# Attention and two expert layers on one core: blocks ordered by pairs of sequences, the second layer's weights converted during the first layer's second block

## The chip, the cores and the metric

The kernel runs on one core of a Trainium2 chip. The time is the device time of one execution in microseconds (us); lower is better. The profiled execution has a span of its own, from its first to its last instruction. The engines are TensorE (PE in the rows, its weight loads PEld), VectorE (DVE), ScalarE (ACT), GpSimd (POOL) and SyncE (SP), which issues nearly all DMAs.

## What is computed

Four sequences of 576 rows, eight heads of width 64, then two layers of width 512 to 2048 and back:

```python
scores = q @ k.T / sqrt(64)
thresh = max(scores, row) - tau
attn = softmax(where(scores >= thresh, scores, -1e9))
x = concat_heads(attn @ v)                    # 2304 x 512
h = x @ moe_w_in                              # first layer
x = (h * clip(h + 3, 0, 6) / 6) @ moe_w_out
h = x @ moe2_w_in                             # second layer
out = max(h, 0) ** 2 @ moe2_w_out
```

The four weight matrices arrive as 64-bit floats, and the results are wanted in float32.

## The kernel before

**Precision.** TensorE multiplies halves: each float32 operand of the layers and of attn @ v is kept as a pair of float16 tiles (a head and the rest), and three products of them are summed. The scores of sequence 0 are plain float32 products (line 281, `u.plain`, set on line 182); those of sequences 1 to 3 use float32r tiles `q_st` and `k_st`, which `prep_steps` fills with a head and a rest of q and k (lines 210, 211, 220 and 221, and a copy by DMA on line 224) and whose products line 285 sums.

**Attention.** A unit is a pair of heads of one sequence, four units to a sequence, nine jobs to a unit: one job is 128 query rows against 576 keys (the ninth takes the last 64 rows of both heads). `scores` fills a PSUM tile, `soft1` takes the row minimum on VectorE (291), the threshold, and the exponent on ScalarE (301); `soft2` applies the threshold on VectorE (308), rounds on ScalarE (314), takes the rest on GpSimd (315, 316) and has a DMA transpose it (318); `av`, `LAG` = 5 steps later, multiplies by v. A generator makes one such step at a time; `attn_to(n)` runs it up to step n.

**Layers.** A block is one layer of one sequence: 16 `hidden` steps and 16 `output` steps (four groups of four), each 24 matmuls with 288 columns (lines 655 and 692). Hidden PSUM tiles, output PSUM tiles and score tiles share one pool of three. Two yields follow each step, and the main loop calls `attn_to` at each, so that attention for the sequence that comes next is spread evenly over the yields that are left until it is needed (`ng`, line 776 onwards). At the end of a first-layer block the largest value of the result is found (line 700 to 707: VectorE, a small matmul, VectorE) and `split_scaled` makes the float16 pairs for the second layer from it.

**Order of blocks.** `blocks` on line 750: for each sequence the first layer, then the second. `BUBBLE` = 8 extra yields stand after a first-layer block, in which attention can run while the split is made. Between a second-layer block and the next sequence's first layer `before_last` finishes attention and calls `split_x`.

**Weights.** A weight unit is 256 rows or columns of a matrix, 32 units in all, used in the order of `wseq`. When sequence 0 needs a unit, `w_next` loads its 1 MB (499 or 502), takes the largest exponent per group of two units (518), makes float32 of the 64-bit words (581 and 589 on ScalarE, 590 on VectorE; the first four units use 584 and 585), rounds to float16 (592), takes the rest on GpSimd (593), and writes the pair to DRAM (595); sequences 1 to 3 read that back (572). `tick` asks for the units `LEAD` steps ahead of use. So both layers' weights are converted in blocks 1_0 and 2_0 (layer and sequence), while the attention of sequence 1 runs.

**Scheduling.** The order of the code gives priorities; the order on each engine is fixed when the program is built.

Of the kernel before, what the change touches and what calls it, by code (L numbers as in the profile page):

```python
# [26 lines left out]
SPLIT = 34  # L27
FIRST_DVE = 4
N_G, N_PT = 3, 5
NWD, N_W = 4, 4  # L30
LEAD = 8
BUBBLE = 8
# [4 lines left out]
def attention_moe_moe_kernel(  # L37
# [52 lines left out]
    q_st = [[big.tile([P, QZ], F32R, name=f"q_st{h}{i}") for i in range(2)] for h in range(2)]  # L90
    k_st = [[big.tile([P, 2, S], F32R, name=f"k_st{h}{i}") for i in range(2)] for h in range(2)]
    own = [slice(0, D), slice(D, 2 * D)]
    xr = [big.tile([P, S], F32, name=f"xr{c}") for c in range(NC)]
# [11 lines left out]
    q_pl = me.tile([P, 2, 2 * NT + 1, P], F32, name="ya", bufs=1)  # L105
    xh, xl = [None] * NC, [None] * NC
    xsc = {}

    def new_x(c):
        t = big.tile([P, 2, S], F16, tag=f"xh{c}", name=f"x16{c}")  # L110
        xh[c], xl[c] = t[:, 0], t[:, 1]
# [13 lines left out]
    def setup():  # L125
# [9 lines left out]
        nc.vector.memset(ones_r, 1.0)  # L135
        for h in range(2):
            nc.gpsimd.memset(q_pl[own[1 - h], :, h * NT:h * NT + NT], 0.0)
            nc.gpsimd.memset(q_pl[own[1 - h], :, 2 * NT, own[h]], 0.0)
        for h in range(2):
            for i in range(2):  # L140
                nc.gpsimd.memset(q_st[h][i][:, NT * P:NT * P + 64].bitcast(F32), 0.0)
                nc.gpsimd.memset(q_st[h][i][:, QZ - 64:].bitcast(F32), 0.0)
        for h in range(2):
            for i in range(2):
                nc.gpsimd.memset(k_st[h][i][own[1 - h], 1, :].bitcast(F32), 0.0)

# [33 lines left out]
    def prep_steps(u):  # L180

        u.plain = u.b == 0
        if u.plain:

            u.qf = q_pl[:, u.i % 2]
            u.kf = xr[2 + u.i % 2]
# [15 lines left out]
            return  # L202
        u.qs = [q_st[h][u.i % 2] for h in range(2)]
# [149 lines left out]
    def finish(u, half):  # L353
# [8 lines left out]
        direct = u.b == 0 and u.p == NC - 1  # L362
        if direct and half == 0:
            new_x(u.p)
        for r, c, src in parts:
            if direct:
                s = xsc["s"]
                nc.scalar.activation(out=xh[u.p][r, c], in_=src, func=AF.Copy, scale=s[r])
                nc.vector.scalar_tensor_tensor(out=xl[u.p][r, c], in0=src, scalar=s[r], in1=xh[u.p][r, c], op0=ALU.mult, op1=ALU.subtract)
            else:  # L370
                nc.scalar.activation(out=xr[u.p][r, c], in_=src, func=AF.Copy)

    def split_scaled(src, s, cs=range(NC)):
        for c in cs:
            new_x(c)
            nc.scalar.activation(out=xh[c], in_=src[c], func=AF.Copy, scale=s)
            nc.vector.scalar_tensor_tensor(out=xl[c], in0=src[c], scalar=s, in1=xh[c], op0=ALU.mult, op1=ALU.subtract)  # L377

    def split_x(b, cs=range(NC)):
        s = xsc["s"] = st.tile([P, 1], F32, name="sx", bufs=2)  # L380
        e = st.tile([P, 1], F32, name="ex", bufs=2)
        nc.vector.tensor_reduce(out=s, in_=vscs[b], axis=AX.X, op=ALU.min)
        nc.vector.reciprocal(out=e, in_=s)
        xsc["e"] = e
        split_scaled(xr, s, cs)
# [34 lines left out]
    def run(us, all_jobs, pr):  # L420
        n = len(all_jobs)
        for i in range(n + LAG):
# [17 lines left out]
            if 0 <= x < n:  # L440
# [42 lines left out]
    n_ld = [0]  # L483
    n_sp = [0]
    w16s = {}
    scaled = {}

# [3 lines left out]
    def w_load():  # L491

        k = n_ld[0]
        src, kind, u, layer, b = wseq[k]
# [10 lines left out]
    def group_scale(k):  # L505

        src, kind, u, layer, b = wseq[k]
# [41 lines left out]
    def norm_scale(q):  # L549
# [3 lines left out]
        ops = [(u, j) for u in range(q * n, q * n + n) for j in range(UW // P)]  # L553
        for i, (u, j) in enumerate(ops):
            w = w_hl[wuse[("2_0", "i", u)]][:, 0, j * P:j * P + P]
            nc.tensor.matmul(a[:, 0:P], lhsT=w, rhs=w, start=i == 0, stop=i == len(ops) - 1)
        am = st.tile([P, 1], F32, name="gm", bufs=2)
        nc.vector.tensor_reduce(out=am, in_=a[:, 0:P], axis=AX.X, op=ALU.max)
        nc.vector.tensor_scalar(out=am, in0=am, scalar1=2.0 ** -40, scalar2=None, op0=ALU.max)  # L559
        m = all_max(am, ident_g)  # L560
        c = slice(q, q + 1)
# [4 lines left out]
    def w_next():  # L566
        k = n_sp[0]
        n_sp[0] += 1
        src, kind, u, layer, b = wseq[k]
        if b:  # L570
            w = new_w(kind)
            nc.sync.dma_start(out=w, in_=w16s[(layer, kind, u)])
            w_hl[k] = w
            return
# [4 lines left out]
        c = wt.tile([P, UW], F32, name="wc", bufs=2)  # L579
        t = wt.tile([P, UW], F32, name="wraw", bufs=2)  # L580
# [10 lines left out]
        w = new_w(kind)  # L591
# [4 lines left out]
        w16s[(layer, kind, u)] = dr  # L596
        w_hl[k] = w
        while n_ld[0] < len(wseq) and wseq[n_ld[0]][4] == 0 and len(w_raw) < NWD:
            w_load()
        n = NQ // UC  # L600
        if k + 1 < len(wseq) and wseq[k + 1][4] == 0 and wseq[k + 1][2] % n == 0:
            group_scale(k + 1)
        if layer == 2 and kind == "i" and u % n == n - 1:
            norm_scale(u // n)
# [17 lines left out]
    def moe(tag, layer, b, before_last):  # L622
# [47 lines left out]
        def output(qd):  # L670
# [151 lines left out]
```

## Time and profile of the kernel before

| | |
|---|---|
| median of 3 runs | 1113.68 us (1111.06 to 1116.08) |
| profiled execution | 1113.99 us, of it the span 1112.0 us |
| PE busy | 1014.1 us, 91% of the span |
| ACT, DVE, POOL busy | 656.2 us (59%), 645.1 us (58%), 501.1 us (45%) |
| DMA, mean share of 16 engines (queue q1) | 61.0% |
| granted TensorE clock, mean | 0.971 of full speed |

The shares are means over stages that differ. A stage is read from the busy times within its own window, set beside the length of that window; a window in which PE is busy throughout can only become shorter by less work for PE.

### The profile page before, as it was taken

How to read it: one execution, taken by the hardware profiler on the slowest of the kernel's cores; microseconds unless marked ns; L12 is line 12 of the kernel's file. 1: busy time of each engine (PE TensorE's matmuls, PEld its weight loads, DVE VectorE, ACT ScalarE, POOL GpSimd, SP SyncE). 2: the span in 40 equal slices, each digit the busy share in tenths (PEclk: the TensorE clock that was granted, in tenths of full speed). 3: DMA queues.
4: the chain of work that ended last, by engine and by line, in shares of the span. 5: the costliest groups of instructions: out<-in, count | busy, mean ns of one | idle time of the engine just before them, and what ended most of it. 6: DMA issues, size and time to landing. Idle time of an engine off the chain costs nothing.

```text
span 1112.0 us, 23377 instructions
## 1 busy us (share of the span) xinstructions
PE 1014.1 (91%) x9248; PEld 820.7 (74%) x9248; DVE 645.1 (58%) x1344; ACT 656.2 (59%) x1128; POOL 501.1 (45%) x613
## 2 busy tenths in 40 slices
PE   6666878898689899999999999999899999998998
PEld 4444666676578788888778888888788887776776
DVE  5878688788876765455765554555934241224122
ACT  6688699687698765655576555655554344313322
POOL 6677467565375743444354443344354212212111
PEclk9989999999799899999999999999999999998999
DMA  6999999888688775565666655656455442322211
GB/s 146 246 230 200 209 263 285 209 236 227 165 213 226 181 171 152 138 151 116 145 138 141 143 131 156 137 119 131 91 113 123 111 125 90 96 76 77 76 39 44
DMA packets 264126, 168.66 MB, mean 152 GB/s; under 512 B 221264, under 2 KB 233552, under 8 KB 264016
## 3 DMA queue, kind: packets, MB, share of 16 engines
q1 hardware_dynamic: 262688, 166.83, 61.0%
q8 instruction: 73, 1.20, 0.4%
q10 hardware_dynamic: 1328, 0.33, 0.1%
q14 instruction: 37, 0.30, 0.1%
HBM read 99.62 MB, written 21.50 MB: 109 GB/s over the span
## 4 chain that ended last, share of the span: by engine, by line
PE 69%; DVE 13%; DMA 9%; ACT 5%; issue 2%; POOL 1%; SPq 1%; DVEq 0%; ACTq 0%; POOLq 0%
PE y L692 29%; PE hp L655 28%; PE s L285 4%; PE o L340 3%; DMA wd<-in_moe_w_out_dram 3%; DMA wd<-in_moe_w_in_dram 3%; DVE wraw L590 2%; DVE nm L291 2%; DVE g L518 1%; DVE x L377 1%; DMA vraw<-in_v_dram 1%; PE tps L174 1%; PE s L281 1%; DVE e L308 1%; ACT wc L581 1%
## 5 line engine op out<-in xcount | busy, mean ns | idle before, releaser
L655 PE MATMUL hp<-x,wpi 128*128 128x288 f16 x3072 | 400.5, 288 | 12.6 <-DVE gm L559 4.2
L655 PEld LDWEIGHTS <-wpi 128*128 128x128 f16 x3072 | 298.6, 99 | 90.9 <-issue 9.0
L692 PEld LDWEIGHTS <-wpo 128*128 128x128 f16 x3072 | 299.3, 99 | 84.3 <-issue 5.4
L692 PE MATMUL y<-gh,wpo 128*128 128x288 f16 x2048 | 338.6, 289 | 7.6 <-DVE ya L698 4.0
L666 POOL TENSOR_TENSOR gl<-g,gh 128x576 f16<-128x576 f32 x128 | 167.4, 1309 | 297.8 <-ACT gh L665 294.3
L692 PE MATMUL y<-gl,wpo 128*128 128x288 f16 x1024 | 209.6, 288 | 0.0
L291 DVE TENSOR_REDUCE nm<-s 128x1 f32<-128x576 f32 x144 | 107.8, 751 | 65.8 <-PE s L285 59.4
L698 DVE SCALAR_TENSOR_TENSOR ya<-y,yq,ya 128x576 f32<-128x576 f32 (+1 forms) x97 | 77.9, 809 | 103.0 <-PE y L692 102.6
L316 POOL TENSOR_TENSOR p<-e,p 128x512 f16<-128x512 f32 x108 | 127.1, 1177 | 0.0
L665 ACT ACTIVATE gh<-g 128x576 f16<-128x576 f32 x128 | 86.9, 680 | 60.4 <-DVE g L663 32.0
L308 DVE SCALAR_TENSOR_TENSOR e<-s,thr,e 128x576 f32<-128x576 f32 x108 | 88.0, 815 | 38.4 <-ACT e L301 37.6
L285 PE MATMUL s<-k_st,q_st 128*128 128x288 f32 x480 | 95.2, 321 | 14.4 <-DVE mx L123 5.3
L340 PE MATMUL o<-v,pt 128*128 128x64 f16 (+1 forms) x2016 | 91.4, 200 | 12.0 <-DMA pt<-wpo 6.4
L314 ACT ACTIVATE p<-e 128x576 f16<-128x576 f32 x108 | 73.5, 681 | 47.9 <-DVE e L308 43.8
L340 PEld LDWEIGHTS <-pt 128*128 128x128 f16 x2016 | 80.9, 101 | 23.7 <-DMA pt<-wpo 9.6
L315 POOL TENSOR_TENSOR p<-e,p 128x64 f16<-128x64 f32 x108 | 39.0, 362 | 118.6 <-issue 82.7
L663 DVE TENSOR_TENSOR g<-g,hp 128x576 f32<-128x576 f32 x64 | 48.1, 751 | 70.8 <-ACT g L662 70.2
L659 ACT ACTIVATE g<-hp,r_h,aq 128x576 f32<-128x576 f32 x64 | 52.9, 828 | 55.1 <-PE hp L655 51.9
L285 PEld LDWEIGHTS s<-k_st,q_st 128*128 128x128 f32 x480 | 70.3, 192 | 18.8 <-issue 11.9
L660 DVE SCALAR_TENSOR_TENSOR g<-g,r_w,hp 128x576 f32<-128x576 f32 x64 | 51.7, 809 | 54.8 <-ACT g L659 54.7
L662 ACT ACTIVATE g<-hp,r_w 128x576 f32<-128x576 f32 x64 | 47.0, 734 | 58.0 <-PE hp L655 57.6
L301 ACT ACTIVATE e<-s,nm 128x576 f32<-128x576 f32 x108 | 78.4, 726 | 0.4
(124 smaller groups left out, 1084.8 us busy)
## 6 DMA issues: line engine op xcount, KB each, us to landing
wpi<-scr SPq DMA_DIRECT2D x48, 512.0 KB, 3.8
wpo<-scr SPq DMA_DIRECT2D x48, 512.0 KB, 3.9
wd<-in_moe_w_in_dram SPq DMA_DIRECT2D x16, 1024.0 KB, 6.9
wd<-in_moe_w_out_dram SPq DMA_DIRECT2D x16, 1024.0 KB, 7.0
scr<-wpi SPq DMA_DIRECT2D x16, 512.0 KB, 5.2
scr<-wpo SPq DMA_DIRECT2D x16, 512.0 KB, 5.7
kraw<-in_k_dram SPq DMA_DIRECT2D x16, 256.0 KB, 4.1
vraw<-in_v_dram SPq DMA_DIRECT2D x16, 256.0 KB, 3.3
```

Source lines behind the costliest of these rows:

```text
L285: nc.tensor.matmul(s[:, half, 0:HALF], lhsT=u.qs[sl][:, cs], rhs=u.ks[sl][:, kk, c], start=i == 0, stop=i == len(ops) - 1)
L291: nc.vector.tensor_reduce(out=j.nm, in_=j.s, axis=AX.XY, op=ALU.min)
L301: nc.scalar.activation(out=j.e, in_=j.s, func=AF.Exp, bias=j.nm, scale=-1.0)
L308: nc.vector.scalar_tensor_tensor(out=j.e, in0=j.s, scalar=j.thr, in1=j.e, op0=ALU.is_le, op1=ALU.mult, accum_out=u.sm[:, col:col + 1])
L314: nc.scalar.activation(out=p16[:, 0:S], in_=e, func=AF.Copy)
L316: nc.gpsimd.tensor_tensor(out=p16[:, S + TAIL:], in0=e[:, 0:NT * P], in1=p16[:, 0:NT * P], op=ALU.subtract)
L340: nc.tensor.matmul(o[:, n * w:n * w + w], lhsT=j.pt[:, c, :], rhs=vv[:, hs, vc, :], start=i == 0, stop=i == len(ops) - 1)
L655: nc.tensor.matmul(hp[:, a, 0:HALF], lhsT=wsl(tag, "i", f, w, c), rhs=x[c][:, a * HALF:(a + 1) * HALF], start=i == 0, stop=i == 3 * NC - 1)
L665: nc.scalar.activation(out=gh, in_=gf, func=AF.Copy)
L666: nc.gpsimd.tensor_tensor(out=gl, in0=gf, in1=gh, op=ALU.subtract)
L692: nc.tensor.matmul(a[:, k_, 0:HALF], lhsT=wsl(tag, "o", f, w, e), rhs=g[f][:, k_ * HALF:(k_ + 1) * HALF], start=i == 0, stop=i == len(ops) ...
L698: nc.vector.scalar_tensor_tensor(out=y, in0=av_, scalar=yq, in1=y, op0=ALU.mult, op1=ALU.add)
```

## The change

It reorders the blocks: both first layers of sequences 0 and 1, then both second layers, then the same for sequences 2 and 3. All attention of sequence 1 must therefore be done within block 1_0, that of sequence 2 within 1_1, 2_0 and 2_1, that of sequence 3 within 1_2; blocks 1_3, 2_2 and 2_3 have none beside them.

The second layer's weights are no longer converted when sequence 0 needs them: `convert` is called for one unit every 2.7 steps from step 34 on (`CONV`; block 1_1 starts at step 32), into a tile `wv` of its own with a single buffer, and only goes to DRAM; the second layer reads all its weights back, for sequence 0 too (16 more reads of 512 KB). Sequence 1's scores become plain float32 like those of sequence 0; the plain tiles and the float32r tiles share their memory, the latter being set up at sequence 2. Two sets of x tiles replace one; x of a sequence is split as soon as its third unit is finished, and the fourth unit's result is written split. `BUBBLE`, `SPLIT` and `before_last` go. Transposed tiles have 6 buffers in place of 5, raw weight tiles 3 in place of 4, and the conversion works in place in one tile (`wc`, 3 buffers). The norm of the second layer's input weights is taken unit by unit.

```diff
-SPLIT = 34
+CONV = (34, 2.7)
-N_G, N_PT = 3, 5
-NWD, N_W = 4, 4
+N_G, N_PT = 3, 6
+NWD, N_W = 3, 4
-BUBBLE = 8
...
+    def split_tiles(i):
         for h in range(2):
...
+            q_st[h][i] = big.tile([P, QZ], F32R, tag=f"qs{h}{i}", name=f"q_st{h}{i}")
+            k_st[h][i] = big.tile([P, 2, S], F32R, tag=f"ks{h}{i}", name=f"k_st{h}{i}")
...
-        u.plain = u.b == 0
+        u.plain = u.b < 2
...
-        direct = u.b == 0 and u.p == NC - 1
+        direct = u.p == NC - 1
...
+                    if j.last and j.u.p == NC - 2:
+                        split_x(j.u.b)
...
-        w = new_w(kind)
+        w = new_w(kind) if layer == 1 else wt.tile([P, 2, UW], F16, name="wv", bufs=1)
         nc.scalar.activation(out=w[:, 0], in_=t, func=AF.Copy)
         nc.gpsimd.tensor_tensor(out=w[:, 1], in0=t, in1=w[:, 0], op=ALU.subtract)
         dr = scr.tile([P, 2, UW], F16, name=f"scr{k}")
         nc.sync.dma_start(out=dr, in_=w)
...
+    def w_next():
+        k = n_sp[0]
+        n_sp[0] += 1
+        src, kind, u, layer, b = wseq[k]
+        if k < len(cseq) // 2:
+            w_hl[k] = convert()
+            return
+        w = new_w(kind)
+        nc.sync.dma_start(out=w, in_=w16s[(layer, kind, u)])
         w_hl[k] = w
...
+        while n_cv[0] < len(cseq) and n_cv[0] >= len(cseq) // 2 and CONV[0] + CONV[1] * (n_cv[0] - len(cseq) // 2) <= step:
+            convert()
...
-            if last and layer == 1 and b < B - 1:
-                for _ in range(BUBBLE):
-                    yield
...
-    blocks = [(f"{layer}_{b}", layer, b) for b in range(B) for layer in (1, 2)]
+    blocks = [(f"{layer}_{b}", layer, b) for p in range(0, B, 2) for layer in (1, 2) for b in (p, p + 1)]
...
+    cseq += [w for w in wseq if w[4] == 0]
```

The order on ScalarE within the first group of outputs of block 1_0, before: `ya` is an output step, `e` the exponent of a job, `wc` and `wpi` passes of a conversion, `q_st` the split of q.

```order
L696 ACTIVATE ya<-y,yq 128x576 x2
L592 ACTIVATE wpi<-wraw 128x1024
L220 ACTIVATE q_st_91<-tps,qs 64x64
L314 ACTIVATE p_2200<-e 128x576
L295 ACTIVATE thr<-nm,tau_a 128x1
L301 ACTIVATE e<-s,nm 128x576
L589 ACTIVATE wd<-wd 128x1024
L220 ACTIVATE q_st_93<-tps,qs 64x256
L581 ACTIVATE wc<-wd,sp 128x1024 x2
L696 ACTIVATE ya<-y,yq 128x576
```

The same place in the changed kernel:

```order
L723 ACTIVATE ya<-y,yq 128x576
L325 ACTIVATE p_2302<-e 128x576
L199 ACTIVATE k_pl_126<-tps 128x256
L199 ACTIVATE k_pl_126<-tps 128x320
L606 ACTIVATE wpo<-wc 128x1024
L306 ACTIVATE thr<-nm,tau_a 128x1
L312 ACTIVATE e<-s,nm 128x576
L606 ACTIVATE wpo<-wc 128x1024
L306 ACTIVATE thr<-nm,tau_a 128x1
L312 ACTIVATE e<-s,nm 128x576
L723 ACTIVATE ya<-y,yq 128x576
```

Between two outputs there were one job's exponent and the split of q; there are now two exponents, and k is only copied (`k_pl`). Of the conversion, two passes stand there where there were four.

The order on VectorE where the last sequence's first layer ends, before: `gm` to `sx` find the scale, `x` are the four splits, `g<-g,hp` on line 663 is the second layer's hidden step.

```order
L703 TENSOR_REDUCE gm<-y_13916 128x1
L118 TENSOR_REDUCE mx<-vm 128x1
L123 TENSOR_SCALAR ex<-mx 128x1
L707 RECIPROCAL sx<-ex 128x1
L629 TENSOR_TENSOR e_14051<-ex 128x1
L679 TENSOR_SCALAR yq<-e_y_109,e_14051 128x1 x3
L377 SCALAR_TENSOR_TENSOR x_14038<-ya,sx,x_14038 128x576
L377 SCALAR_TENSOR_TENSOR x_14041<-ya,sx,x_14041 128x576
L377 SCALAR_TENSOR_TENSOR x_14044<-ya,sx,x_14044 128x576
L377 SCALAR_TENSOR_TENSOR x_14047<-ya,sx,x_14047 128x576
L663 TENSOR_TENSOR g<-g,hp 128x576 x5
```

In the changed kernel sequence 2's first layer ends so, and the hidden steps between and behind (`g<-g,r_w,hp`) are sequence 3's first layer:

```order
L730 TENSOR_REDUCE gm<-y_11776 128x1
L687 SCALAR_TENSOR_TENSOR g<-g,r_w_97,hp 128x576
L121 TENSOR_REDUCE mx<-vm 128x1
L126 TENSOR_SCALAR ex<-mx 128x1
L734 RECIPROCAL s_11890<-ex 128x1
L656 TENSOR_TENSOR e_12924<-ex 128x1
L388 SCALAR_TENSOR_TENSOR x_11898<-ya,s_11890,x_11898 128x576
L388 SCALAR_TENSOR_TENSOR x_11901<-ya,s_11890,x_11901 128x576
L388 SCALAR_TENSOR_TENSOR x_11904<-ya,s_11890,x_11904 128x576
L388 SCALAR_TENSOR_TENSOR x_11907<-ya,s_11890,x_11907 128x576
L687 SCALAR_TENSOR_TENSOR g<-g,r_w_97,hp 128x576 x3
```

The splits moved from standing ahead of the hidden steps that need them to standing among the hidden steps of another sequence.

The order on ScalarE early in block 1_1 of the changed kernel (before, this block has no conversion beside it): `g` and `gh` are hidden steps, `wc` and `wv` the second layer's conversion.

```order
L686 ACTIVATE g<-hp,r_h,aq 128x576
L692 ACTIVATE gh<-g 128x576
L595 ACTIVATE wc<-wd,sp 128x1024 x2
L686 ACTIVATE g<-hp,r_h,aq 128x576
L606 ACTIVATE wv<-wc 128x1024
L306 ACTIVATE thr<-nm,tau_a 128x1
L312 ACTIVATE e<-s,nm 128x576
L221 ACTIVATE k_st_3497<-tps 64x320
L692 ACTIVATE gh<-g 128x576
```

The conversion's passes stand between the two ScalarE operations of hidden steps, in one in-order queue.

## Rows read from the trace of the kernel before

**Rows 1.** Busy time by stretch: start:end, length, then engines as the first line says

```profile
core 0: us, PE busy (x) PEld busy (x) DVE busy (x) ACT busy (x) POOL busy (x), PEclk, DMA share, GB/s
0.00:118.40 118.40, 78.94 (x657) 56.47 (x657) 89.95 (x211) 88.78 (x176) 80.37 (x153) 0.91 0.92 204
118.40:435.80 317.40, 275.92 (x2538) 224.21 (x2538) 241.12 (x517) 241.88 (x384) 183.46 (x187) 0.95 0.83 214
435.80:678.20 242.40, 237.20 (x2292) 197.03 (x2290) 140.54 (x298) 143.53 (x264) 103.81 (x128) 1.00 0.60 140
678.20:914.10 235.90, 232.48 (x2244) 192.80 (x2243) 121.27 (x246) 124.98 (x225) 92.59 (x113) 0.99 0.52 119
914.10:1112.00 197.90, 189.54 (x1524) 150.21 (x1522) 52.24 (x77) 56.99 (x79) 40.83 (x32) 0.98 0.23 73
```

**Rows 2.** The same view for seven quarters of blocks, and for the end

```profile
163.80:206.40 42.60, 34.12 (x302) 27.13 (x302) 36.99 (x72) 36.73 (x52) 31.25 (x29) 0.92 1.04 288
238.00:293.20 55.20, 40.12 (x357) 32.80 (x354) 45.77 (x98) 39.51 (x58) 29.86 (x33) 0.87 0.83 231
372.40:401.90 29.50, 29.50 (x292) 24.60 (x291) 19.24 (x43) 17.64 (x30) 19.85 (x21) 1.00 0.77 180
732.20:761.10 28.90, 28.90 (x286) 23.86 (x285) 15.00 (x30) 13.99 (x23) 13.90 (x17) 1.00 0.57 120
761.10:798.60 37.50, 35.56 (x370) 30.56 (x369) 27.81 (x67) 23.04 (x47) 14.34 (x21) 0.95 0.64 137
956.80:980.30 23.50, 23.50 (x194) 18.77 (x193) 6.53 (x8) 6.05 (x8) 5.10 (x4) 1.00 0.29 90
1081.10:1112.00 30.90, 26.01 (x213) 20.79 (x211) 7.98 (x11) 6.65 (x10) 3.83 (x3) 1.00 0.13 39
```

**Rows 3.** Lines 291 and 581 in five such quarters; last, 581 from 118.4 to 435.8

```profile
L291 DVE TENSOR_REDUCE nm<-s x5: 737/758/758, 164.5 to 199.6; 128x1 f32<-128x576 f32 x5
L581 ACT ACTIVATE wc<-wd,sp x6: 1225/1240/1255, 163.3 to 192.9; 128x1024 f32<-128x1024 f32 x6
L291 DVE TENSOR_REDUCE nm<-s x9: 740/747/758, 238.9 to 286.9; 128x1 f32<-128x576 f32 x9
L581 ACT ACTIVATE wc<-wd,sp x6: 1232/1244/1253, 238.9 to 276.1; 128x1024 f32<-128x1024 f32 x6
L291 DVE TENSOR_REDUCE nm<-s x5: 747/752/758, 376.3 to 401.7; 128x1 f32<-128x576 f32 x5
L581 ACT ACTIVATE wc<-wd,sp x2: 1229/1240/1252, 377.9 to 379.0; 128x1024 f32<-128x1024 f32 x2
L291 DVE TENSOR_REDUCE nm<-s x5: 747/748/758, 736.1 to 760.5; 128x1 f32<-128x576 f32 x5
L291 DVE TENSOR_REDUCE nm<-s x8: 737/747/757, 760.5 to 793.4; 128x1 f32<-128x576 f32 x8
L581 ACT ACTIVATE wc<-wd,sp x28: 1201/1237/1262, 137.4 to 379.0; 128x1024 f32<-128x1024 f32 x28
```

**Rows 4.** Groups of instructions by line: the three passes of one weight conversion on ScalarE

```profile
L581 ACT ACTIVATE wc<-wd,sp 128x1024 f32<-128x1024 f32 x32 | 37.9, 1234 | 0.2
L589 ACT ACTIVATE wd<-wd 128x1024 int32<-128x1024 uint16 x28 | 32.3, 1155 | 12.0 <-DMA wd<-in_moe_w_out_dram 8.4 <-DMA wd<-in_moe_w_in_dram 3.4
L592 ACT ACTIVATE wpi<-wraw 128x1024 f16<-128x1024 f32 x16 | 16.7, 1050 | 0.6 <-DVE wraw L590 0.6
```

**Rows 5.** Timeline of TensorE: eight float32 score records (281), eight of the split form (285)

```profile
33.13 2.11 PE L281 MATMUL s<-xr,ya 128*128 128x288 f32 x8
223.80 1.31 PE L285 MATMUL s<-k_st,q_st 128*128 128x288 f32 x8
```

**Rows 6.** Groups by line: VectorE's half of the split of q

```profile
L221 DVE SCALAR_TENSOR_TENSOR q_st<-tps,qs,q_st 64x256 fp32r<-64x256 f32 x72 | 30.0, 417 | 15.0 <-ACT q_st L220 13.0
```

**Rows 7.** Groups by line and DMA issues: the tail of a conversion

```profile
L593 POOL TENSOR_TENSOR wpi<-wraw,wpi 128x1024 f16<-128x1024 f32 x16 | 34.1, 2136 | 5.8 <-ACT wpi L592 5.4
scr<-wpi SPq DMA_DIRECT2D x16, 512.0 KB, 5.2
```

More of the change, by code (lines that the diff above doesn't have):

```diff
@@ L89, in attention_moe_moe_kernel @@
     QZ = NT * P + 3 * 64
-    q_st = [[big.tile([P, QZ], F32R, name=f"q_st{h}{i}") for i in range(2)] for h in range(2)]
-    k_st = [[big.tile([P, 2, S], F32R, name=f"k_st{h}{i}") for i in range(2)] for h in range(2)]
+    q_st = [[None] * 2, [None] * 2]
+    k_st = [[None] * 2, [None] * 2]
+    q_pl = [None] * 2
+    k_pl = [None] * 2
     own = [slice(0, D), slice(D, 2 * D)]
-    xr = [big.tile([P, S], F32, name=f"xr{c}") for c in range(NC)]
+    xr = [big.tile([P, S], F32, name=f"xr{c}") for c in range(NC - 1)]
     NG = NF // NQ
@@ L102, in attention_moe_moe_kernel, with new_x @@
     ident_g = const.tile([P, P], F32, name="ident_g")
[L105 to L111, printed above, removed]
+    X, xsc, xset = {}, {}, {}
+    def new_x(key, c):
+        if key not in X:
+            xset[key] = len(X) % 2
+            X[key] = [None] * NC, [None] * NC
+        t = big.tile([P, 2, S], F16, tag=f"x{xset[key]}{c}", name=f"x16{c}")
+        X[key][0][c], X[key][1][c] = t[:, 0], t[:, 1]
+        return X[key][0][c], X[key][1][c]
     def all_max(am, rhs=None):
@@ L483, in attention_moe_moe_kernel @@
     n_ld = [0]
+    n_cv = [0]
     n_sp = [0]
@@ L493, in w_load @@
         k = n_ld[0]
-        src, kind, u, layer, b = wseq[k]
+        src, kind, u, layer, b = cseq[k]
         n_ld[0] += 1
@@ L505, in group_scale @@
     def group_scale(k):
-        src, kind, u, layer, b = wseq[k]
+        src, kind, u, layer, b = cseq[k]
         n = NQ // UC
@@ L547, in group_scale, with norm_scale @@
         return sp
-    def norm_scale(q):
+    n2 = {}
+    def norm_scale(u, w):
         n = NQ // UC
         a = ps_a.tile([P, 512], F32, tag="acc", name="gr")
[L553 to L556, printed above, removed]
+        for j in range(UW // P):
+            v = w[:, 0, j * P:j * P + P]
+            nc.tensor.matmul(a[:, 0:P], lhsT=v, rhs=v, start=j == 0, stop=j == UW // P - 1)
+        if u % n == 0:
+            n2[0] = st.tile([P, n + 1], F32, name="n2", bufs=2)
+            nc.gpsimd.memset(n2[0][:, n:], 2.0 ** -40)
+        nc.vector.tensor_reduce(out=n2[0][:, u % n:u % n + 1], in_=a[:, 0:P], axis=AX.X, op=ALU.max)
+        if u % n < n - 1:
+            return
         am = st.tile([P, 1], F32, name="gm", bufs=2)
-        nc.vector.tensor_reduce(out=am, in_=a[:, 0:P], axis=AX.X, op=ALU.max)
-        nc.vector.tensor_scalar(out=am, in0=am, scalar1=2.0 ** -40, scalar2=None, op0=ALU.max)
+        nc.vector.tensor_reduce(out=am, in_=n2[0], axis=AX.X, op=ALU.max)
         m = all_max(am, ident_g)
-        c = slice(q, q + 1)
+        c = slice(u // n, u // n + 1)
         unit_of(m, m)
@@ L564, in norm_scale, with convert @@
         nc.vector.tensor_scalar(out=a_w[1][:, c], in0=m, scalar1=e_w[1][:, c], scalar2=2.0 ** 21, op0=ALU.mult, op1=ALU.mult)
[L566 to L570, printed above, removed]
-            w = new_w(kind)
-            nc.sync.dma_start(out=w, in_=w16s[(layer, kind, u)])
-            w_hl[k] = w
-            return
+    def convert():
+        k = n_cv[0]
+        n_cv[0] += 1
+        src, kind, u, layer, b = cseq[k]
         while n_ld[0] <= k:
@@ L596, in w_next @@
         w16s[(layer, kind, u)] = dr
-        w_hl[k] = w
[L598 to L604, printed above, removed]
+        while n_ld[0] < len(cseq) and len(w_raw) < NWD:
+            w_load()
+        if k + 1 < len(cseq) and cseq[k + 1][2] % (NQ // UC) == 0:
+            group_scale(k + 1)
+        if layer == 2 and kind == "i":
+            norm_scale(u, w)
+        return w
+    def w_next():
[4 more added lines that the diff above has]
+            w_hl[k] = convert()
+            return
+        w = new_w(kind)
+        nc.sync.dma_start(out=w, in_=w16s[(layer, kind, u)])
+        w_hl[k] = w
     def want_w(k):
@@ L779, in attention_moe_moe_kernel @@
                 break
-            ng += 4 * NF + (BUBBLE if t[0] == "1" else 0)
+            ng += 4 * NF
         start = steps[0]
-        xs = None
-        if i + 1 < len(blocks) and blocks[i + 1][1] == 1:
-            def xs(nxt=nxt, b=b):
-                attn_to(nxt + LAG)
-                split_x(b + 1)
-        for g, _ in enumerate(moe(tag, layer, b, xs)):
+        for g, _ in enumerate(moe(tag, layer, b)):
             if nxt is not None:
                 attn_to(min(nxt + LAG, start + math.ceil((nxt + LAG - start) * (g + 1) / ng)))
+        if i + 1 < len(blocks) and blocks[i + 1][1] == 1:
+            attn_to(nxt + LAG)
 _INS = ['q', 'k', 'v', 'tau', 'moe_w_in', 'moe_w_out', 'moe2_w_in', 'moe2_w_out']
```

77 lines of the change are left out of this document (38 added, 39 removed).

## The prediction

> **What bounds the kernel now.** The page's mean, TensorE busy for 91% of the span, hides two regimes, so I read busy times by stretch first: the start, then four pairs of blocks (both layers of one sequence) [rows 1]. The start, sequence 0's attention alone, takes 118.4 us with TensorE busy for 78.94 of it. The first pair takes 317.4 us and the second 242.4, though both do the same matrix work. The reader is to see the difference in the other columns: in the first pair ScalarE is busy for 241.88 us and VectorE for 241.12, against 143.53 and 140.54 in the second, because the weights of both layers are converted there. TensorE is busy for 237.20 of the second pair's 242.4 us and sets its length; in the first pair nothing is full, and everything waits a little for everything. The last pair has no attention and takes 197.9 us.
>
> Next come quarters of blocks, cut at every 192nd matrix product of the layers [rows 2], with two counts that tell what else ran in them [rows 3]. A bare quarter takes 23.5 us. With five jobs of attention it takes 28.9, TensorE being busy throughout: a job costs it (28.9 - 23.5) / 5 = 1.08 us. With eight jobs it takes 37.5, and TensorE is idle at times: (37.5 - 28.9) / 3 = 2.9 us for each job more. With five jobs and two conversions it takes 29.5, with five and six 42.6, with nine and six 55.2. So conversions cost 0.3 us each as long as TensorE is full, (42.6 - 28.9) / 6 = 2.3 us each when it isn't. In the quarters of 42.6 and 55.2 us the busiest engine, VectorE, is busy for 36.99 and 45.77 us, 87% and 83%. That share is my measure of how full such a mix gets.
>
> **The change, part by part.** The new order makes five stretches: the start; A, block 1_0 with all attention of sequence 1; B, blocks 1_1, 2_0 and 2_1 with that of sequence 2 and the second layer's conversion; C, block 1_2 with that of sequence 3; D, blocks 1_3, 2_2 and 2_3 alone.
>
> *The start.* The same steps come before the first block, and the same three units of weights are asked for: 118.4 us, as before. One raw weight buffer less and one transposed tile more I cost at nothing: what hides them is that a load is issued two units ahead; without it each late load would show as idle time of VectorE or ScalarE ahead of a conversion.
>
> *Plain scores for sequence 2 of the four.* Eight float32 records take 2.11 us on TensorE, eight of the split form 1.31 [rows 5], 0.264 and 0.164 us each with their ends. A unit has 36 of the one or 40 of the other: 9.5 against 6.6 us, so four units cost TensorE about 11.8 us more. In return VectorE loses its half of the split: for q alone 30.0 us over three sequences, 10 for one [rows 6], and the copies by DMA go.
>
> *A.* Its loop makes 41 steps of attention in one block where 128 yields used to share them. ScalarE's work is what it had in the first pair, 241.88 us, less a second-layer block (half of the last pair's 56.99, so 28.5), less the conversions that leave: 27 started in that stretch [rows 3], and of the first layer's 16 about 12 stay, so 15 go at 1.234 + 1.155 + 1.050 = 3.44 us [rows 4], 51.6. That leaves 162 us; VectorE loses the same parts and the split besides. At 86% full A takes 162 / 0.86 = 188 us. The bounds: 162, if ScalarE never waits; and by the slopes above, 10.25 jobs and 3 conversions a quarter, 4 x (28.9 + 5.25 x 2.9 + 3 x 2.3) = 204, with the 11.8 on top 216. I take 188, because the loaded quarters kept to that share with as many conversions and more.
>
> *B.* Twelve quarters with 3 steps of attention each: 12 x (23.5 + 3 x 1.08) = 321 us. The 16 conversions lie beside work of TensorE; at 0.3 us each B takes 326, at 2.3 us 358. There are about three to a quarter, between the cases of two and six, and their outgoing tile has one buffer; I take 1.2 us each, 340 us. The 16 reads more of 512 KB are hidden by the lead of eight steps.
>
> *C.* 31 jobs and the steps that trail them in four quarters, nearly eight to each: 4 x 37.5 = 150 us. The bounds: 4 x (23.5 + 7.75 x 1.08) = 127, if TensorE stays full; and the quarter with nine jobs and six conversions, less 2.3 for each of these, 4 x 41.4 = 166. I take the row that has the same mix. That row, TensorE at 35.56 of 37.5 us where it was full with five jobs, says that packing jobs costs only some 5% of TensorE's time. The Trainium skill (Perfetto Trace Analysis, section Optimization Strategy) speaks against the change here: a kernel whose most-contended engine changes from regime to regime may gain by interleaving the regimes, and this one takes attention out of three blocks and packs it into two. By that rule A and C would lie at their upper bounds, and the sum would be 44 us higher.
>
> *D.* Twelve bare quarters, and what the last one takes more than a bare one: 12 x 23.5 + (30.9 - 23.5) = 289.4 us, and 2.6 for the transposes of the other result: 292. The scale and the split between a sequence's two layers, which nothing covered in the last pair, now lie beside another sequence's hidden steps. Upper bound: one and a half times the last pair's 197.9, 297.
>
> *The sum.* 118.4 + 188 + 340 + 150 + 292 = 1088.4 us of span, with the 2.0 us that the profiled execution has around its span **1090 us**, against that execution's 1113.99; the median of the runs, 1113.68, is the same within 0.3 us, so nothing is shifted. The first two sequences go from 317.4 + 242.4 = 559.8 us to 528, the last two from 433.8 to 442: the gain is in taking 15 conversions out of a stretch where nothing is full and laying them under TensorE; a part is given back in C and by the plain scores.
>
> **The rivals.**
>
> 1. *Packed attention stalls TensorE (slower).* Scores, hidden and output tiles share three PSUM tiles, so a score tile that waits for VectorE holds up the next block step. At the upper bounds A is 216 and C 166: 1134 us. For it: the slope of 2.9 us a job, nearly three times TensorE's own 1.08. The Trainium skill's rule named above (Perfetto Trace Analysis, Optimization Strategy) would bring this. Against it: 95% in the quarter with eight jobs, and a VectorE that has less to do per job. It decides as soon as A and C together cost over 24 us more than forecast. Chance 0.16.
> 2. *The single outgoing buffer.* Rounding 1.05, the rest on GpSimd 2.14 and the landing of the write 5.2 us [rows 4, 7] make 8.4 us before the next conversion may round; 2.7 steps of B at 26.7 / 8 us are 9.0. Whatever delays one by over 0.6 us stops ScalarE, and behind it the hidden steps' own operations. At 2 us for each of 15 the time is 1120. Against it: stalls of ScalarE in single places are made up for as long as TensorE has a tile to go on with. Chance 0.10.
> 3. *Everything fits (faster still).* A at ScalarE's 162 and B at 326: 1050 us. For it: TensorE's own work in A is only 4 x 23.5 + 41 x 1.08 + 11.8 = 150 us; against it: no loaded quarter was over 87% full. Chance 0.14.
> 4. *The change doesn't do what it says*: the conversions could slip back behind their due times. The order has them in block 1_1. 0.02; about 1114 us.
>
> **How the numbers follow.** The forecast has a chance of 0.58, and by itself lies between 1072 and 1108, by A's share between 0.83 and 0.95 and B's conversions between 0.3 and 2.3. The range 1062 to 1124 takes in that, most of rival 2 and the nearer parts of 1 and 3. About 0.5%, 5.6 us, is what a measurement of this kernel can tell from no change. Faster than 1108 are most of the forecast and rival 3, with milder cases of rival 2: 0.68. The near misses of the forecast and of rival 2 make 0.13, rivals 1 and the worse half of 2, with what the forecast leaves over, 0.19.
>
> **What would show it.** In the changed profile: the start at 118 us; block 1_0 from its first matrix product of line 682 to the next block's in about 188 us, the busiest engine at 83 to 90%; block 1_1 to 2_1 near 340 with TensorE at 95% or more; 1_2 about 150; the last three blocks at 23.5 us a quarter without a gap. If A is over 212 us, or if ScalarE waits long before the rounding into `wv`, the forecast is wrong; if D isn't free of gaps, its simplest part is.

## The result and the profile after

The changed kernel takes 1122.05 us (median of 9 runs, 1116.47 to 1129.63), the one before 1111.83 us beside it (9 runs, 1107.31 to 1116.08): a ratio of 1.0088, 95% interval 1.0067 to 1.011. It is slower by 0.9%, where 1090 us and a gain were forecast: inside the range, near its upper end, on the side that had a chance of 0.19.

The changed kernel's page, busy time by engine (us, share of the span, instructions): by the sums of [rows 1], TensorE is busy for 12.6 us more than before and ScalarE for 10.7 less, in a span of 1123.9 us (the profiled execution took 1125.69 us in all).

```profile
PE 1026.7 (91%) x9232; PEld 823.3 (73%) x9232; DVE 627.9 (56%) x1317; ACT 645.5 (57%) x1117; POOL 498.1 (44%) x621
```

Busy times of the changed kernel in the prediction's five stretches, the start, A (block 1_0), B (1_1, 2_0, 2_1), C (1_2) and D (1_3, 2_2, 2_3); the columns are those of [rows 1]:

```profile
0.00:116.30 116.30, 79.30 (x643) 57.81 (x644) 83.82 (x198) 86.12 (x171) 77.36 (x153) 0.88 0.88 195
116.30:331.80 215.50, 180.18 (x1623) 139.76 (x1623) 159.01 (x356) 167.08 (x296) 127.97 (x158) 0.95 0.89 216
331.80:690.00 358.20, 342.80 (x3160) 280.46 (x3158) 210.69 (x436) 211.17 (x346) 159.07 (x166) 1.00 0.65 175
690.00:831.50 141.50, 136.96 (x1462) 115.08 (x1461) 92.51 (x206) 92.57 (x182) 72.45 (x97) 1.00 0.61 135
831.50:1123.90 292.40, 287.43 (x2350) 230.20 (x2348) 81.83 (x122) 88.59 (x124) 61.28 (x48) 0.99 0.26 84
```

| stretch | forecast | measured | difference |
|---|---|---|---|
| start | 118.4 | 116.3 | -2.1 |
| A | 188 | 215.5 | +27.5 |
| B | 340 | 358.2 | +18.2 |
| C | 150 | 141.5 | -8.5 |
| D | 292 | 292.4 | +0.4 |
| span | 1088.4 | 1123.9 | +35.5 |

D is what was forecast, with TensorE busy for 287.43 of 292.4 us: the stop between a sequence's two layers is gone. The stretches here begin with a block's first matrix product; [rows 1] ends its pairs some 5 us later, when the next block already runs. Cut in both kernels at the first product of block 1_2, the two halves are, first before, then changed:

```profile
118.40:672.90 554.50, 507.82 (x4784) 416.75 (x4784) 379.31 (x809) 383.55 (x646) 287.27 (x315) 0.97 0.73 182
672.90:1112.00 439.10, 427.32 (x3810) 347.51 (x3807) 175.86 (x325) 183.83 (x307) 133.43 (x145) 0.99 0.39 100
116.30:690.00 573.70, 522.98 (x4781) 420.22 (x4781) 369.70 (x792) 378.25 (x642) 287.04 (x324) 0.98 0.74 191
690.00:1123.90 433.90, 424.40 (x3810) 345.29 (x3808) 174.34 (x328) 181.16 (x306) 133.72 (x145) 1.00 0.37 101
```

C and D together gained 5.2 us, A and B lost 19.2. Of these, 15.2 us are time in which TensorE is busy (522.98 for 507.82); its idle time there grew by 4.0. So the question is what A and B lost. In A ScalarE is busy for 167.08 us, close to the 162 of the forecast's sum, but that is 78% of the block's length and not 86%. The busiest engine of A is TensorE: 180.18 us, 84%, where the prediction had 150 for it (*rival 3*). Most of TensorE's idle time in A, some 23 of 35.3 us, ended when VectorE had read a hidden tile (line 687) or a score tile (line 319), which share the three PSUM tiles; the longest waits (engine, line, what it waited for: us in total, times, the longest):

```profile
PE hp L682 <- DVE g L687: 10.7, 4, 3.9
PE s L292 <- DVE e L319: 5.5, 5, 2.3
PE o L351 <- DMA pt<-p: 3.8, 3, 2.6
PE y L719 <- DVE e L319: 2.9, 1, 2.9
```

ScalarE's waits in A name three candidates for what comes late: rounded tiles that can't be written because their transposes have not been read out, raw weights that are late, and VectorE's row minimum.

```profile
ACT p L325 <- DMA pt<-p: 8.5, 6, 2.9
ACT wd L603 <- DMA wd<-in_moe_w_in_dram: 7.0, 5, 3.0
ACT thr L306 <- DVE nm L302: 4.5, 5, 2.2
```

### The profile page after: what moved, and what is told of

The parts are those of the page before. It is cut to its first block, busy times and chain, and to the rows that moved or that the text cites. A ratio compares the mean times of both kernels' runs of the same rounds, so it can differ in the third digit from the quotient of the medians.

```text
span 1123.9 us, 23296 instructions
## 1 busy us (share of the span) xinstructions
PE 1026.7 (91%) x9232; PEld 823.3 (73%) x9232; DVE 627.9 (56%) x1317; ACT 645.5 (57%) x1117; POOL 498.1 (44%) x621
## 4 chain that ended last, share of the span: by engine, by line
PE 55%; DMA 16%; DVE 11%; ACT 9%; POOL 3%; issue 3%; SPq 2%; ACTq 0%; POOLq 0%; DVEq 0%
PE y L719 26%; PE hp L682 23%; DMA wd<-in_moe_w_in_dram 5%; DMA pt<-p 4%; DMA scr<-wv 2%; DMA wd<-in_moe_w_out_dram 2%; PE o L351 2%; PE s L296 2%; PE s L292 2%; ACT p L325 1%; DVE wc L604 1%; DMA vraw<-in_v_dram 1%; DVE nm L302 1%; DVE e L319 1%; DVE x L388 1%
## 5 line engine op out<-in xcount | busy, mean ns | idle before, releaser
L292 PE MATMUL s<-k_pl,q_pl 128*128 128x288 f32 x288 | 93.7, 457 | 25.8 <-DVE g L319 14.3
L351 PE MATMUL o<-v,pt 128*128 128x64 f16 (+1 forms) x2016 | 88.3, 198 | 13.7 <-DMA pt<-wpo 4.5
L292 PEld LDWEIGHTS s<-k_pl,q_pl 128*128 128x128 f32 x288 | 54.9, 209 | 43.4 <-DVE g L319 12.1
L326 POOL TENSOR_TENSOR p<-e,p 128x64 f16<-128x64 f32 x108 | 34.8, 322 | 110.9 <-ACT p L325 48.6
```

Source lines behind the costliest of these rows:

```text
L292: nc.tensor.matmul(s[:, half, 0:HALF], lhsT=u.qf[:, t, :], rhs=u.kf[:, c], start=True, stop=True)
L351: nc.tensor.matmul(o[:, n * w:n * w + w], lhsT=j.pt[:, c, :], rhs=vv[:, hs, vc, :], start=i == 0, stop=i == len(ops) - 1)
```

## The experiments

Theories on record ahead of the runs: L, raw weights come late, since the change has one raw buffer less; P, the plain scores cost TensorE what made A long; W, the single outgoing buffer `wv` holds the conversions up; M, the mix in A is too dense; T, the tiles of attention hold it up. Times are medians, each with the ratio to the kernel before on the same chip; runs with a profile alone say so. Stretches are from the profiled execution, cut in each kernel at its own matrix products.

### Raw weights, plain scores, the place of the conversions

The kernel before with three raw buffers:

```diff
-NWD, N_W = 4, 4
+NWD, N_W = 3, 4
```

> The kernel before with three raw weight buffers in place of four, nothing else. Theory L (raw weights arrive late because the change has one raw buffer less): slower than before by 8 to 20 us, in the first pair of blocks. Theory M (the mix of attention, conversion and matrix work in block 1_0 is simply too dense for the in-order engines): within 3 us of before.

1113.41 us, ratio 1.0015 (0.9996 to 1.0034). In the kernel before, the buffer is worth nothing that can be measured, as the prediction had it.

The changed kernel without most loads of raw weights:

```diff
         n_ld[0] += 1
-        t = wt.tile([P, UW, 2], I32, name="wd", bufs=NWD)
+        if k >= NWD:
+            w_raw[k] = raw0[k % NWD]
+            return
+        t = raw0[k] = wt.tile([P, UW, 2], I32, name="wd0", bufs=NWD)
```

> The changed kernel without the loads of raw weights behind the third: 29 of 32 loads of 1 MB are left out and the first three tiles are converted again and again, so the output is not the reference's; result tiles have one buffer of their own. Theory L: block 1_0 falls from 215 to 195 us or less, the six quarters with conversions behind it from 193 to about 175, 1085 us in all. Theory M: block 1_0 stays above 207 us.

1121.25 us, ratio 1.0079 (1.0058 to 1.01). Its A, B and C:

```profile
117.30:329.10 211.80, 178.63 (x1642) 140.25 (x1639) 158.85 (x351) 165.32 (x298) 130.34 (x157) 0.95 0.64 139
329.10:675.50 346.40, 340.06 (x3160) 279.69 (x3159) 207.31 (x435) 211.00 (x346) 162.98 (x167) 1.00 0.57 148
675.50:818.80 143.30, 137.34 (x1462) 115.00 (x1460) 91.99 (x206) 92.43 (x183) 72.37 (x97) 1.00 0.63 134
```

The DMA share of A (last column but one) falls from 0.89 to 0.64, and A only from 215.5 to 211.8 us: theory L falls for A; of the 7.0 us of waits for raw weights above, 3.7 us of block came back. B falls by 11.8 us; of that the loads may have a part (ScalarE waits for raw weights for 22.0 us in B of the changed kernel), but D is 7 us longer in this build, which has a single result buffer, so the total tells little.

The changed kernel with sequence 1's scores in the split form:

```diff
-        u.plain = u.b < 2
+        u.plain = u.b == 0
```

> The changed kernel with sequence 1's scores in the split form again (plain for sequence 0 alone). Theory P (plain scores cost TensorE what made block 1_0 long): 12 us or more faster, all of it in block 1_0. Theories L and M: TensorE gains 12 us but VectorE, ScalarE and the DMA queue get the split's work back, so block 1_0 stays within 5 us of 215.

1136.96 us, ratio 1.0229 (1.0204 to 1.0255): 15 us slower than the changed kernel, so theory P falls; in this build the plain scores are a gain. Its A:

```profile
122.40:336.00 213.60, 171.16 (x1624) 135.05 (x1625) 167.24 (x377) 167.45 (x296) 122.31 (x149) 0.93 0.94 220
```

TensorE is busy there for 171.16 us in place of 180.18, 9 us less (the prediction had 11.8; over the whole span it is 5), and VectorE for 167.24 in place of 159.01; the block is nearly as long. The start is 6 us longer in this build (122.4 us); the profile shows no place for the remainder.

The changed kernel with the second layer's conversion when block 2_0 needs it:

```diff
-        w = new_w(kind) if layer == 1 else wt.tile([P, 2, UW], F16, name="wv", bufs=1)
+        w = new_w(kind)
...
-        if k < len(cseq) // 2:
+        if b == 0:
             w_hl[k] = convert()
...
-        while n_cv[0] < len(cseq) and n_cv[0] >= len(cseq) // 2 and CONV[0] + CONV[1] * (n_cv[0] - len(cseq) // 2) <= step:
-            convert()
```

> The changed kernel with the second layer's weights converted when block 2_0 needs them, into the ordinary weight tiles, in place of beside block 1_1 into a tile of one buffer; 16 reads back fewer. Theory W (the single outgoing buffer holds up the conversions): blocks 1_1 to 2_1 fall from 358 to 345 us or less. If the conversions cost their 2 us each wherever they lie beside matrix work: 358 within 5, only shifted by a block. Block 1_0 stays at 215 by all theories.

1117.98 us, ratio 1.0048 (1.0026 to 1.007), some 4 us faster than the changed kernel. Its B:

```profile
331.20:683.00 351.80, 340.68 (x3160) 279.73 (x3158) 212.97 (x436) 213.67 (x347) 162.80 (x168) 1.00 0.58 156
```

6.4 us shorter, where theory W wanted 13 or more. In B of the changed kernel ScalarE's wait for the write that frees `wv` is short:

```profile
ACT wv L606 <- DMA scr<-wv: 6.8, 2, 4.4
```

The buffer and the 16 reads more cost a little at most, as 4 us is less than two builds of A differ by (below); the conversions cost nearly the same in both places.

### What the conversions cost

In three kernels conversions were left out, with their loads, passes, writes and reductions (the small work on scales stays); where a block needs the unit, a ready tile is read:

```diff
+        if left_out(k):
+            w16s[(layer, kind, u)] = w16s[(1, kind, u % 2)]
+            if layer == 1:
+                w = new_w(kind)
+                nc.sync.dma_start(out=w, in_=w16s[(1, kind, u % 2)])
...
+            return w
```

> The changed kernel with 10 of the first layer's conversions left out (those behind the sixth: their loads, passes, write and the reductions of their scales; a ready tile is read from DRAM in their place, so the output is not the reference's). Theory M (dense mix): without them block 1_0 is what attention and matrix work make of it, about 172 us as 1_2 with ten jobs more and plain scores would be: 215 - 43, 4 us for each conversion. Theory S (the 41 steps of attention alone fill block 1_0): above 200 us.

> The changed kernel with all 16 conversions of the second layer left out in the same way, and the matrix products of their norm (output not the reference's). If they cost the prediction's 1.2 us each or less: blocks 1_1 to 2_1 fall from 358 to 339 at the lowest. If 2 us each, as the quarters of the changed profile say: 326 us. Block 1_0 stays at 215.

> The kernel before with the 26 conversions behind the sixth left out in the same way (output not the reference's). The first pair of blocks falls from 317 to about 242, the second pair's length, if its whole excess is the conversions (2.9 us each); to 265 or more if a part is something else that the change should have removed.

One run each. Without ten of the first layer's, 1094.3 us; its A and C:

```profile
115.60:304.90 189.30, 171.30 (x1623) 136.28 (x1623) 137.51 (x335) 136.69 (x266) 102.33 (x148) 0.98 0.87 191
658.70:800.10 141.40, 136.93 (x1463) 115.06 (x1461) 92.60 (x206) 92.88 (x182) 72.42 (x97) 1.00 0.64 135
```

A is 189.3 us: 26.2 less, 2.6 for a conversion. That lies between the two theories. The conversions are dear, and without most of them A is still 14 us longer than the 175 that C with ten jobs more, plain scores and no conversion would make (141.5 + 10 x 1.08 + 11.8, plus some 10 for the conversions left).

Without the second layer's, 1093.38 us; its B:

```profile
322.30:657.70 335.40, 333.90 (x3087) 275.02 (x3086) 177.93 (x383) 171.94 (x306) 125.46 (x155) 1.00 0.52 129
```

B falls by 22.8 us, 1.4 for a conversion, close to the 1.2 of the prediction; A falls too, to 205.0, as the first loads, reductions and passes of the second layer stand in it. Over the whole span, 1123.9 against 1091.5 us, it is 2.0 for a conversion. What is left of B, 335.4, is 14 us over the 321 that the forecast had for its jobs and matrix work, and TensorE is busy for 333.90 of it.

The kernel before without 26 of them, 1064.63 us; its first and second pair, and under it the first pair of the kernel before, cut at the same products:

```profile
119.30:383.10 263.80, 250.23 (x2411) 206.88 (x2408) 172.83 (x435) 161.94 (x304) 120.04 (x168) 0.99 0.66 151
383.10:625.30 242.20, 238.27 (x2292) 198.46 (x2291) 140.62 (x297) 143.30 (x265) 103.74 (x128) 0.99 0.63 141
```

```profile
118.40:430.50 312.10, 270.62 (x2495) 219.71 (x2495) 238.74 (x512) 240.06 (x382) 183.46 (x187) 0.95 0.83 214
```

The first pair falls from 312.1 to 263.8 us, 1.9 for a conversion, but not to the second's 242.2. So two thirds of its excess were conversions; 21.6 us remain that my reading had put down to them as well. Two conversions are left in that pair, some 4 us; and TensorE is busy there for 12 us more than in the second pair (250.23 against 238.27), so the two aren't alike for it.

### The tiles of attention

The changed kernel with a third buffer for the rounded tiles:

```diff
-            p16 = at.tile([P, 2 * S], F16, name="p16")
+            p16 = at.tile([P, 2 * S], F16, name="p16", bufs=3)
```

> The changed kernel with three buffers in place of two for the rounded tiles that wait for their DMA transpose. Theory T (ScalarE's waits of 8.5 us for transposes in block 1_0 hold the block up): 6 us or more faster, in block 1_0. Theory M: the waits move elsewhere, within 3 us of the changed kernel.

1106.97 us, ratio 0.9938 (0.992 to 0.9956): 15 us faster than the changed kernel, and faster than the one before. Its A, B and C:

```profile
115.00:320.30 205.30, 178.27 (x1624) 139.62 (x1623) 161.00 (x355) 165.98 (x294) 125.46 (x157) 0.94 0.93 226
320.30:678.40 358.10, 346.24 (x3160) 282.48 (x3158) 210.18 (x438) 213.74 (x348) 160.79 (x167) 0.98 0.66 175
678.40:814.70 136.30, 135.72 (x1462) 115.02 (x1461) 93.15 (x206) 93.64 (x182) 72.25 (x97) 1.00 0.66 140
```

C falls from 141.5 to 136.3 us, with TensorE at 135.72 of it, and A from 215.5 to 205.3. ScalarE's longest waits in C, first in the changed kernel, then in this one:

```profile
ACT p L325 <- DMA pt<-p: 12.9, 9, 3.8
ACT g L686 <- PE hp L682: 5.6, 3, 2.8
```

```profile
ACT p L325 <- DVE e L319: 7.8, 13, 1.2
ACT thr L306 <- DVE nm L302: 7.1, 11, 1.3
```

12.9 us of waiting for transposes (line 325 can't round a job before the transpose of two jobs ago is through) are gone from the list; what leads now is the wait for VectorE.

Is it the buffer, or the order? Each edit makes the scheduler build another order, so the pair was repeated in two other kernels: without ten conversions, and with five buffers for transposed tiles (`N_PT`).

> The changed kernel without 10 of the first layer's conversions (as in the earlier run, output not the reference's) and with three buffers for the rounded tiles. If the two buffers hold the attention of block 1_0 up by themselves: the block falls from 189 to 180 us or less, and 1_2 from 141.5 to 136. If what a third buffer gave in block 1_0 was the conversions' doing or another order of the scheduler: 186 or more, and only 1_2 falls.

> The changed kernel with five buffers for the transposed tiles as before the change, in place of six. If the sixth mattered: 3 us or more slower. If it didn't, the same within 2 us but for what another order of the scheduler makes of block 1_0, which this run then bounds.

> The same with three buffers for the rounded tiles. If the gain of the third is of the tiles and not of the order drawn: faster than the one before by 10 us or more, 5 of them in 1_2. If block 1_0's part was the order: by about 5 us, all in 1_2.

Without ten conversions and with three buffers (one run, 1079.04 us), A and C:

```profile
114.40:294.30 179.90, 168.34 (x1624) 135.52 (x1624) 137.75 (x335) 135.07 (x264) 102.72 (x148) 0.99 0.94 200
648.50:784.80 136.30, 135.70 (x1463) 115.06 (x1461) 93.47 (x206) 93.53 (x182) 72.29 (x97) 1.00 0.65 141
```

ScalarE's wait for transposes in A, with two buffers and with three:

```profile
ACT p L325 <- DMA pt<-p: 14.6, 13, 2.6
ACT p L325 <- DMA pt<-p: 2.1, 2, 1.8
```

Against 189.3 and 141.4 with two, the blocks are 9.4 and 5.1 us shorter: in this pair of builds the two tiles held up the attention packed into A, with few conversions beside it, and into C, with none. With five transposed tiles, first with two buffers (1123.52 us, ratio 1.0102, 1.0053 to 1.0151), then with three (1123.08 us, ratio 1.0075, 1.0041 to 1.0109):

```profile
118.70:324.90 206.20, 177.15 (x1616) 137.68 (x1612) 161.63 (x354) 166.32 (x295) 125.38 (x156) 0.96 0.89 224
685.80:826.70 140.90, 137.00 (x1463) 115.14 (x1461) 92.54 (x206) 92.74 (x182) 72.42 (x97) 1.00 0.63 136
```

```profile
119.80:328.10 208.30, 177.35 (x1615) 138.79 (x1612) 163.30 (x352) 165.16 (x292) 125.94 (x155) 0.95 0.93 222
690.00:826.50 136.50, 135.77 (x1463) 115.04 (x1461) 93.17 (x206) 93.66 (x182) 72.27 (x97) 1.00 0.67 140
```

C again falls by 4.4 us, but A doesn't, though 7.4 us of ScalarE's waits for transposes are gone from it, and the total hardly. A of the changed work is 206.2 us in this order with two buffers and 215.5 in the other. So C's 5 us are shown (140.9 to 143.3 us in all seven kernels of this order with two buffers, 136.2 to 136.5 in all six with three or more), and A's 9 in the one pair in which most conversions are out; in A with all its conversions the buffer can't be told from what one build and execution differs by from another, which is about as much.

The kernel before with the third buffer:

> The kernel before with three buffers for the rounded tiles that wait for their transpose. If two buffers bind only where attention is packed (theory T, as the change packs it): within 4 us of before, since its attention is spread thinner. If they bind the kernel before as well, a part of what the change lost was never its own: 8 us or more faster.

1107.99 us, ratio 0.9955 (0.9941 to 0.9969), 5 us faster: between the two readings. A part of the shortage was there before.

### Versions that beat both

> The changed kernel with both edits that helped: three such buffers, and the second layer's weights converted when block 2_0 needs them. If the two gains (15 and 4 us) are separate: 1103 us. If the conversions in 2_0 fall on the same limit: 1107 or more.

The third buffer and conversions at use: 1104.52 us, ratio 0.9919 (0.9894 to 0.9945), about the sum of the two gains. With a third buffer for the exponents as well:

```diff
-            j.e = at.tile([P, 2, HALF], F32, name="e", bufs=2)
+            j.e = at.tile([P, 2, HALF], F32, name="e", bufs=3)
```

> As the one before, with three buffers in place of two for the float32 exponents too. If the chain of attention tiles is still what holds block 1_0: 5 us or more faster than it. If the engines' mix is (theory M): the same within 3 us.

1094.93 us, ratio 0.9833 (0.9807 to 0.9859), the fastest. Its five stretches:

```profile
0.00:111.90 111.90, 77.62 (x644) 56.51 (x645) 84.07 (x198) 85.78 (x172) 77.37 (x153) 0.89 0.90 201
111.90:310.50 198.60, 175.05 (x1623) 138.15 (x1623) 160.72 (x356) 163.99 (x294) 124.64 (x156) 0.97 0.99 233
310.50:664.80 354.30, 342.75 (x3161) 280.76 (x3159) 213.15 (x437) 214.60 (x349) 163.14 (x168) 1.00 0.58 155
664.80:801.10 136.30, 135.73 (x1463) 115.05 (x1461) 93.39 (x206) 93.46 (x182) 72.25 (x97) 1.00 0.67 141
801.10:1093.50 292.40, 287.38 (x2350) 230.18 (x2347) 81.85 (x122) 88.60 (x124) 61.28 (x48) 1.00 0.27 84
```

C and D are as in the kernel with three and two; A is 198.6 us where that one had 207.5, the start 111.9 where it had 115.0. Two controls followed: a fourth buffer for the rounded tiles, and the same tiles in the order of blocks from before the change (there with one raw weight buffer less, to make room).

> The changed order with conversions at use, three buffers for the exponents and four for the rounded tiles. If the chain of attention tiles still holds block 1_0 (198 us with three and three): 3 us or more faster than 1095 us. If the engines' mix does by now: the same within 2 us.

> The kernel before with three buffers for the exponents and three for the rounded tiles, paid for with one raw weight buffer (which cost nothing measurable by itself). If the order by pairs is worth something once the tiles of attention are not short: slower than the same tiles in the changed order (1095 us) by 5 us or more. If the order is worth nothing and the tiles are all: 1098 us or less.

The fourth buffer: 1104.8 us, ratio 0.9928 (0.9906 to 0.9951), where three had 0.9833. Its A and C (the profiled execution took 1109.79 us, the longest of its runs):

```profile
117.00:328.10 211.10, 179.18 (x1624) 140.03 (x1624) 161.14 (x356) 167.07 (x295) 124.81 (x157) 0.94 0.93 218
679.30:815.60 136.30, 135.71 (x1462) 115.04 (x1460) 93.13 (x206) 93.51 (x182) 72.18 (x97) 1.00 0.67 141
```

C is the same 136.3 us, and D the same 292.4; the start and A are 17.6 us longer than above, 117.0 and 211.1 us against 111.9 and 198.6. I know no way in which one more buffer could hold that chain up. The instructions of TensorE, ScalarE, VectorE, GpSimd and SyncE stand in the same order in both kernels until A has begun, and yet the start differs by 5.1 us. Its second and third part, first with three buffers, then with four (the last column but two is the granted clock):

```profile
40.00:80.00 40.00, 23.86 (x190) 16.59 (x190) 34.82 (x78) 28.37 (x54) 24.51 (x42) 0.85 0.99 260
80.00:111.90 31.90, 25.09 (x265) 19.10 (x264) 23.34 (x58) 29.48 (x64) 26.26 (x43) 0.87 1.00 187
```

```profile
40.00:80.00 40.00, 25.74 (x196) 17.74 (x195) 33.43 (x78) 27.57 (x52) 23.53 (x43) 0.82 0.98 250
80.00:111.90 31.90, 23.05 (x214) 17.38 (x213) 20.91 (x48) 27.42 (x60) 25.26 (x37) 0.79 0.92 186
```

The granted clock is 0.85 and 0.87 in the one and 0.82 and 0.79 in the other, between the two levels of 1.2 and 2.4 GHz, in stretches in which TensorE has pauses; in A it is 0.97 and 0.93. So the same order ran at two speeds, on two chips on which the kernel before took 1112.81 and 1112.88 us. The fast start is the exception: in four more kernels with this order up to A (the changed one, the one with conversions at use, the one with three rounded tiles, and the one with both edits) the start takes 115.0 to 116.3 us, at a granted clock of 0.79 to 0.81 in its last third. Whether the higher clock made that start short or came of it, no run shows. In A the order differs too, and of the 12.5 us there I can't say what is order and what is clock.

The old order of blocks with three and three: 1112.57 us, ratio 0.9998 (0.9977 to 1.002), no gain. With enough tiles, then, and conversions at use in both, the changed kernel was faster than the old order in each of the two builds that I have of it, by 0.7% and by 1.65%; one build of the old one is little to compare with. Nor is it shown that this is the order's doing: the changed kernel also has plain scores for sequence 1, worth 15 us in the one build without them, and no run has the old order with plain scores.

## Why the prediction was wrong

**A, the step that failed: "at 86% full A takes 162 / 0.86 = 188 us".** It took ScalarE for A's busiest engine, with 162 us, and had 150 for TensorE. ScalarE's work came out nearly right, 167.08 us (the sum takes off one conversion too few: the row has 28 started, not 27, which makes 158), but it filled only 78% of A, and 77 to 83% over the builds with all the work (198.6 to 215.5 us). TensorE was the busiest engine, with 180.18 us and 84%, so the sign "busiest engine at 83 to 90%" came true by another engine and another length. Its idle time, 35.3 us, is about the 38 that 188 leaves beside 150; what the forecast lacked is some 30 us in which TensorE is busy. The rows before had them: by the way in which ScalarE's 162 was found, TensorE's would have been 275.92 less half of 189.54, about 181 us, an estimate from [rows 1] before the plain scores are added and the second layer's norms are taken off. The price of 1.08 us for a job came from a quarter with two of the transposes of q and k; A has 50, and those of the attention's result besides:

```profile
L183 PE MATMUL tps<-ident,qraw 128*128 128x128 f32 x25 | 4.8, 292 | 0.8 <-ACT k_pl L199 0.8
L183 PE MATMUL tps<-ident,kraw 128*128 128x128 f32 x25 | 4.6, 284 | 2.0 <-ACT os L355 1.4 <-DVE os L362 0.3 <-DVE mx L121 0.2
L368 PE MATMUL xT<-ident,os 128*128 128x128 f32 x20 | 4.2, 283 | 0.6 <-ACT os L358 0.6
```

In C with three tiles, where TensorE is full, a job with its share of these costs (135.72 - 4 x 23.5) / 31 = 1.35 us. In A without ten conversions and with three tiles TensorE is still busy for 168.34 us; the other 12 of the 180 go with the conversions and a granted clock of 0.95 for 0.99.

That TensorE's work by itself sets A's length is not shown: with split scores it had 9 us less, and the block was nearly as long. The upper bound from the slopes, 216, lies nearest to the 215.5, with 2.3 us for a conversion where TensorE isn't full (measured in A: 2.6) and 2.9 for a job; as the builds with all the work differ by up to 17 us in A, that it meets this one is in part luck. The two rounded tiles are a part of A's length where few conversions are beside them; what else of it is order, clock and mix stays open.

**B, +18 us.** The conversions' price of 1.2 us each held within B (1.4). The term of the sum that was too small is the other one, "12 x (23.5 + 3 x 1.08) = 321 us": without any conversion B takes 335.4, and TensorE is busy for 333.90 of it. It is the same price of a job that was too small, and the transposes of block 2_0's and 2_1's results were left out. The premise that the excess of the first pair was conversions held for two thirds.

**C and D.** C's row of the same mix gave 150 for 141.5, D 292 for 292.4. Of the rivals' times, 1120 of *rival 2* lies nearest, by luck, as its mechanism is not what cost the time (below). Of *rival 1*, 1134 us, A's half came and C's didn't, and A and C together were 19 us over the forecast, under its mark of 24. Its place was right; TensorE's waits in A end as it says, at VectorE's reads of the three PSUM tiles, but they sum to no more than the forecast's own idle time, and no run changed those tiles. The Trainium skill (Perfetto Trace Analysis, Optimization Strategy) says that a kernel whose most-contended engine changes over time may gain by interleaving those regimes; as the prediction read this, both dense blocks would have lost. The traces agree in A alone, and in C TensorE was busy for 97% of the block, 136.96 of 141.5 us, with 31 jobs packed beside it.

**The rest.** *Rival 2*, the outgoing buffer, is small: at most 4 us of the 30 that it was given. The raw weight buffer cost nothing in the kernel before, as said. The plain scores cost TensorE 9 us in A for 11.8, and paid for them in the one build that tells. The gain from laying conversions under TensorE was nearly all imagined: 2.6 us each in A and 1.4 in B stand against 1.9 in the kernel before, and 12 x 2.6 + 16 x 1.4 = 54 us is no less than 28 x 1.9 = 53.

## What to carry to other kernels

When work is packed more densely, find the work of every engine in the new stretch in the same way, from the same rows, before one of them is taken for the limit: here one subtraction would have given TensorE some 181 us where a price from a thin quarter gave 150. Set beside that the slope between the densest rows. Count the buffers of the tiles in the packed chain: a wait of one engine for a DMA that frees its output tile is the row to look for, and in a block without other load it can be tested alone. Where a scheduler builds the order, one edit can move a dense stretch by as much as the effect looked for, so repeat a pair in a second build before believing it.

## What was not expected

The DMA engines' share in A says little about its length: 0.89 and 0.64 went with blocks of 215.5 and 211.8 us. And one order of instructions took 111.9 us in one kernel and 117.0 in another, at a granted clock of 0.87 and 0.79 in its last third, while the blocks in which TensorE has work without pause, 1_2 to 2_3, agree within 0.1 us.
